# A local-attention and soft-MoE kernel: the output columns of its last stage cut into 384 and 128 in place of 256 and 256, with its steps in another order

## Chip, cores and metric

The kernel runs on one core of one Trainium2 chip. The metric is the device time of one execution in microseconds (us), from the runtime's own measurement; lower is better. Three runs of the kernel before took 188.71 to 189.39 us, with a median of 188.79 us. The core has a matrix engine (TensorE: PE for matmuls, PEld for loading their stationary operand), three engines for elementwise work (VectorE = DVE, ScalarE = ACT, GpSimd = POOL), a queue engine that issues transfers (SyncE = SP) and 16 DMA engines that carry them. Matmuls write PSUM (8 banks of 128 x 512 float32 here), all else lives in SBUF (128 partitions).

## What is computed

Attention with 8 heads over 4 sequences of 768 tokens, where a key is kept if it is one of the first 8 or one of the last 96, with a linear bias by distance; its output, as 3072 tokens of 512 features, goes through a soft mixture of 8 experts with 4 slots each. Only the mixture's end is touched here:

```python
logits = x @ phi                          # 3072 x 32
d = softmax(logits, axis=0)
slot_input = (d.T @ x).reshape(8, 4, 512)
for e in range(8):
    h = np.maximum(slot_input[e] @ w1[e], 0.0)     # 4 x 1024
    slot_out[e] = h @ w2[e]                        # 4 x 512
c = softmax(logits, axis=1)
return c @ slot_out.reshape(32, 512)      # 3072 x 512
```

All is float32. `w1` and `w2` are 16.8 MB each and are read once; the output is 6.29 MB.

## The kernel before

Up to about 136 us the kernel works through 16 units of attention, in the order of the table `ORDER`, while the weights stream into whatever SBUF is free. Then comes a tail that is written out by hand, in the order in which the code stands:

- `Moe.hidden` (line 104): the first projection and its relu, 64 matmuls of 512 columns, four at a time side by side in the array (one per slot of four experts: 128 rows, 32 columns of weights each).
- `Moe.project` (line 144): the second projection, `h @ w2`. It is done in two parts of the 512 output columns, `OUT_PART` (line 45). Part 0 gathers in bank `xx[:, 0]`, part 1 in `xx[:, 1]`. A part has 16 rounds (two halves `a` of the experts, eight chunks `c` of the inner dimension); a round is four matmuls side by side, with the part's width as their moving columns. The trace shows each float32 matmul as two records, so that a round is two passes of four.
- `weights_by_slot` (line 169): seven transposes turn the token weights `c` into `ct`; DVE copies them out of PSUM.
- `slots_raw` (line 179) copies a part's slots out of PSUM (ACT), `slots_spread` (line 183) repeats them over the four groups of 32 partitions with a matmul (tile `sp`) and copies them to `sos`.
- `combine` (line 193): one step is `c @ slot_out` for `k` tiles of 128 tokens in each of four groups, in four PSUM banks `cp`; ACT and DVE copy two banks each to SBUF, and SP issues one output transfer for each pair of banks. `STEPS` (line 46) is the number of tiles in each step.

Small PSUM tiles come from six banks in turn (`LeftBanks`), so a step waits for the copies out of the bank that it takes again. `load_w` (line 399) issues the weights. The last eight pieces of the 32 (24 to 31, the second half of `w2`) go into buffers that still hold first-projection weights, so `reuse_first` and `reuse_second` are called from inside `hidden` and issue them in columns as they come free. All transfers, weights and output, go through SP's one queue in program order, and eight may be outstanding. The fallback `general` is taken only if a flag is set; every engine reads the flag (line 968) and branches at the end.

Of the kernel before, what the change touches and what calls it, by code (L numbers as in the profile page):

```python
# [20 lines left out]
B, H, S, D = 4, 8, 768, 64  # L21
# [3 lines left out]
P = 128  # L25
NJ = 7
# [15 lines left out]
E, SPE, DF = 8, 4, 1024  # L42
NS = E * SPE
HF = DM // 2
OUT_PART = ((0, HF), (HF, HF))
STEPS = ((1, 1, 2, 2), (1, 1, 2, 2))
XH = NJ * HF
TABW = 4 * QW
NW = 10
# [17 lines left out]
class Moe:  # L67
# [69 lines left out]
    def segments(n, c):  # L137

        at, w = OUT_PART[n]
        f = 8 * at + c * w  # L140
# [37 lines left out]

    def slots_raw(self, o, ow):

        self.nc.scalar.copy(out=ow, in_=o[:, 0:ow.shape[1]])

    def slots_spread(self, ps, ow, so, copies):

        nc = self.nc
        m = ow.shape[1] // 2
        for k, copy in enumerate(copies):
            sp = ps.tile([P, 512], F32, name="sp", tag="x")
            c = slice(m * k, m * k + m)
            nc.tensor.matmul(out=sp[:, 0:m], lhsT=self.spread, rhs=ow[:, c], start=True, stop=True)  # L190
            copy(out=so[:, c], in_=sp[:, 0:m])  # L191

    def combine(self, ps, ct, n, so, obs, out, step):


        nc = self.nc
        at, w = OUT_PART[n]
        k, t0 = STEPS[n][step], sum(STEPS[n][:step])
        cps = [ps.tile([P, 512], F32, name="cp", tag="x") for _ in range(B)]
        for h in range(k):  # L200
            for b in range(B):
                r = slice(NS * b, NS * b + NS)
                t = t0 + h
                nc.tensor.matmul(out=cps[b][:, w * h:w * h + w], lhsT=ct[r, P * t:P * t + P], rhs=so[r], start=True, stop=True)  # L204
        for b in range(0, B, 2):
            obs.append(obs.pop(0))
            ob = obs[-1][:, 0:2 * k * w]
            for i, copy in enumerate((nc.scalar.copy, nc.vector.tensor_copy)):
                copy(out=ob[:, k * w * i:k * w * i + k * w], in_=cps[b + i][:, 0:k * w])
            c = B * S // P * at + w * (B * t0 + b * k)  # L210
            nc.sync.dma_start(out=out[:, c:c + 2 * k * w], in_=ob)


class BiasTable:
# [83 lines left out]
def tile_attention_moe(ctx: ExitStack, tc: tile.TileContext, qk, v, phi, w1, w2, nn, out):  # L298
    nc = tc.nc
# [28 lines left out]
    WP = 2048  # L328
    VC, VH = NJ * 2 * D, NJ * (D + 1)
    VV = VH + VC // 2  # L330
    weights = [keep.tile([P, WP], F32, name=f"wp{i}") for i in range(NW)]
# [43 lines left out]
    npl = len(places)  # L375
    extras = []
    for k, n in enumerate(held):
        at = 0
        for c0, c1 in sorted(c for h, *cs in spaces for c in cs if h == n) + [(WP, WP)]:
            if at < c0:  # L380
                extras.append((NW + k, at, c0))
            at = c1
# [4 lines left out]
    def piece(k):  # L387
        m, r = divmod(k, 16)
        if m == 0:
            a, r = divmod(r, 8)  # L390
            half, s = divmod(r, 4)
        else:
            half, r = divmod(r, 8)
            a, s = divmod(r, 4)
        return m, 4 * a + s, half
# [3 lines left out]
    def load_w(pieces, c0=0, c1=WP):  # L399

        for k in pieces:
            m, e, half = piece(k)
            nc.sync.dma_start(out=places[k][:, c0:c1], in_=(w1, w2)[m][e][:, WP * half + c0:WP * half + c1])
# [94 lines left out]
    class LeftBanks:  # L498

        n = 0  # L500
# [368 lines left out]
    ct = ts.tile([P, S], F32, name="ct")  # L869
# [7 lines left out]
    def check_inputs():  # L877

        def reduced(c, rows, x, axes, at_least):
            nc.vector.tensor_reduce(out=fl[0:rows, c:c + 1], in_=x, axis=axes, op=ALU.min)  # L880
            nc.vector.tensor_scalar(out=fl[0:rows, c:c + 1], in0=fl[0:rows, c:c + 1], scalar1=at_least, scalar2=None, op0=ALU.is_ge)

        reduced(1, KB, rsall[:, :, 0:6], AX.XY, RS_MIN)
        reduced(6, TN[6], rsall[0:TN[6], :, 6], AX.X, RS_MIN)
        xt = left.tile([P, 512], F32, name="xt", tag="x")
        nc.tensor.transpose(out=xt[0:B * H, 0:KB], in_=xmax, identity=ident[0:KB, 0:KB])  # L886
        nc.vector.tensor_reduce(out=fl[0:B * H, 5:6], in_=xt[0:B * H, 0:KB], axis=AX.X, op=ALU.max)  # L887
        nc.vector.tensor_scalar(out=fl[0:B * H, 5:6], in0=fl[0:B * H, 5:6], scalar1=X_MIN, scalar2=None, op0=ALU.is_ge)
        reduced(7, KB, cst[:, :, 1], AX.X, 0.5)
        nc.vector.tensor_scalar(out=fl[:, 2:3], in0=nlo, scalar1=1.0, scalar2=None, op0=ALU.is_ge)  # L890
        nc.vector.tensor_scalar(out=fl[:, 3:4], in0=nlo, scalar1=float(WIN), scalar2=None, op0=ALU.is_le)
        nc.vector.tensor_scalar(out=fl[:, 4:5], in0=ngl, scalar1=float(NG), scalar2=None, op0=ALU.is_le)
        nc.vector.tensor_reduce(out=fl[:, 8:9], in_=fl[:, 0:8], axis=AX.X, op=ALU.min)
        nc.vector.tensor_scalar(out=fl[:, 9:10], in0=fl[:, 8:9], scalar1=-1.0, scalar2=-1.0, op0=ALU.add, op1=ALU.mult)

    def set_flag():
        ft = left.tile([P, 512], F32, name="ft", tag="x")
        nc.tensor.matmul(out=ft[0:1, 0:1], lhsT=fl[:, 9:10], rhs=ones[:, 0:1], start=True, stop=True)
        nc.vector.tensor_scalar(out=flag[0:1], in0=ft[0:1, 0:1], scalar1=0.5, scalar2=None, op0=ALU.is_ge)
# [7 lines left out]
    w1_of = lambda e, half: places[where[0, e, half]]  # L907

    def reuse_first():
        load_w(range(npl + 1, npl + 5), 0, WP // 2)  # L910
        load_w(range(npl + 5, 31), 0, WP // 4)

    def reuse_second():
        load_w([31], 0, WP // 4)
        load_w(range(npl + 1, npl + 5), WP // 2, WP)
        load_w(range(npl + 5, 31), WP // 4, WP)

    moe.hidden(left, Moe.slot_view(sl), w1_of, hs, ht, (reuse_first, reuse_second))
    load_w([31], WP // 4, WP)

    obs = [places[16 + i // 2][:, 1024 * (i % 2):1024 * (i % 2) + 1024] for i in range(2 * (npl - 16))]
    ops = [xx[:, n] for n in range(2)]
    parts = [slice(at, at + w) for at, w in OUT_PART]

    def project(n, a, cs=range(8)):
        moe.project(ops[n], ht, lambda e, h: places[where[1, e, h]], n, a, cs)

    def weights(tiles, copy):
        moe.weights_by_slot(left, lnat, ct, [(t, TN[t], KB * t) for t in tiles], copy)

    def slots_raw(n):
        moe.slots_raw(ops[n], ows[:, parts[n]])

    def slots_spread(n, *copies):
        moe.slots_spread(left, ows[:, parts[n]], sos[:, parts[n]], copies)

    def combine(n, *steps):
        for step in steps:
            moe.combine(left, ct, n, sos[:, parts[n]], obs, out, step)

    for a in range(2):
        project(0, a, range(4))
    moe.hidden_t(left, hs, ht, 1)
    check_inputs()
    for a in range(2):
        project(0, a, range(4, 8))
    slots_raw(0)
    weights(range(4), nc.vector.tensor_copy)
    weights(range(4, NJ), nc.vector.tensor_copy)
    slots_spread(0, nc.scalar.copy, nc.scalar.copy)  # L950
    project(1, 0, (0,))
    combine(0, 0, 1)
    project(1, 0, (1, 2, 3))
    combine(0, 2)
    project(1, 0, (4, 5, 6))
    combine(0, 3)
    project(1, 0, (7,))
    project(1, 1)
    slots_raw(1)
    set_flag()  # L960
    slots_spread(1, nc.vector.tensor_copy, nc.scalar.copy)
    combine(1, *range(len(STEPS[1])))
    order.close()
    tail.close()
    banks.close()
# [7 lines left out]
def general(ctx, tc, moe, qk, v, phis, w1, w2, ngl, nlo, ident, out):  # L973
# [114 lines left out]
    with ExitStack() as g3:  # L1088
# [26 lines left out]
        obs = [sb.tile([P, 1024], F32, name=f"gob{i}") for i in range(2)]  # L1115
        for n, (at, w) in enumerate(OUT_PART):
            c = slice(at, at + w)
# [4 lines left out]
            moe.slots_spread(ps, ow[:, c], so[:, c], (nc.vector.tensor_copy, nc.scalar.copy))  # L1122
            for step in range(len(STEPS[n])):
                moe.combine(ps, ct, n, so[:, c], obs, out, step)
# [6 lines left out]
def _layout(q, k, v, n_global, n_local, moe_phi, moe_w1, moe_w2):  # L1131
# [6 lines left out]
    for j in range(NJ):  # L1138
# [11 lines left out]
        "w1": np.asarray(moe_w1, f32).reshape(E, 4, P, DF).transpose(0, 2, 1, 3).reshape(E, P, 4 * DF),  # L1150
        "w2": np.concatenate([w2[..., a:a + w].reshape(E, P, 8 * w) for a, w in OUT_PART], axis=2),
        "n": np.array([[int(n_global), int(n_local)]], np.int64).view(np.int32),
# [28 lines left out]
```

## Time and profile before

| What | Value |
|---|---|
| median of three runs | 188.79 us (188.71 to 189.39) |
| the profiled execution, its own time | 188.87 us |
| its span, first to last instruction | 186.9 us |
| outside the span in that execution | 1.97 us |
| PE busy, share of the span | 169.8 us, 91% |
| DVE, ACT, POOL busy | 142.5, 125.4, 91.6 us |
| DMA mean rate; read, written | 328 GB/s; 54.59 MB, 6.29 MB |
| granted TensorE clock, mean | 0.986 of 2.4 GHz |

Times in the rows are microseconds from the first instruction. Shares are averages over a span with very different stages, so the tail is read by itself: which engine works without a break, when the DMA engines idle, and what the last landing waits for. A matmul's end is modelled, so starts of successive rows say more than durations.

### The profile page before, as it was taken

Reading aid. Unit: us, or ns where it says so; the run is one execution under the profiler, and the core shown is the slowest. Engines: PE = TensorE matmul, PEld = TensorE weight load, DVE = VectorE, ACT = ScalarE, POOL = GpSimd, SP = SyncE. Lnnn points to the kernel's source line nnn. Section 1 sums busy time; section 2 is a strip of 40 time slices with the busy share of each in tenths; the row PEclk is TensorE's granted clock in tenths of the full one; section 3 lists DMA queues with packets and bytes.
Section 4 is the critical chain, followed back from the end, with each engine's and each line's share of the span. In section 5 each row is a group of like instructions: output and inputs, shape, how many; then the busy total and the mean of one; then the engine's idle time right before and its main releaser. Section 6 shows DMA issues by size and latency. Waiting matters only on the chain.

```text
span 186.9 us, 6377 instructions
## 1 busy us (share of the span) xinstructions
PE 169.8 (91%) x2635; PEld 123.7 (66%) x2635; DVE 142.5 (76%) x379; ACT 125.4 (67%) x161; POOL 91.6 (49%) x121
## 2 busy tenths in 40 slices
PE   8899899999998999999999997898899999998900
PEld 2568689887886798888789895584523355554600
DVE  5999999999999999899999899974687002541610
ACT  3499989999987989999999999924102111341610
POOL 6826688868967769569769776700010000000000
PEclk9999999999999999999999999999999999999995
DMA  5999999898998856988986789999999999877592
GB/s 186 419 406 391 407 404 399 335 366 273 375 361 306 329 200 199 365 282 313 312 301 176 247 297 418 349 341 412 408 375 349 404 408 420 319 295 291 222 394 83
DMA packets 14872, 61.38 MB, mean 328 GB/s; under 512 B 1650, under 2 KB 2802, under 8 KB 13042
## 3 DMA queue, kind: packets, MB, share of 16 engines
q1 hardware_dynamic: 14832, 60.89, 86.6%
q8 instruction: 22, 0.36, 0.7%
q14 instruction: 16, 0.13, 0.2%
q10 hardware_dynamic: 2, 0.00, 0.0%
HBM read 54.59 MB, written 6.29 MB: 326 GB/s over the span
## 4 chain that ended last, share of the span: by engine, by line


## 5 line engine op out<-in xcount | busy, mean ns | idle before, releaser
L581 POOL TENSOR_TENSOR ph<-tb,ph 128x432 f16<-128x432 f32 x78 | 82.3, 1085 | 28.1 <-ACT ph L574 26.4
L571 ACT ACTIVATE tb<-tb,nb 128x1296 f32<-128x1296 f32 x32 | 43.5, 1373 | 1.6 <-DVE nb L567 1.5
L598 PEld LDWEIGHTS <-ph 128*128 128x128 f16 x1248 | 41.4, 97 | 3.8 <-issue 3.2
L598 PE MATMUL x<-v,ph 128*128 128x65 f16 (+1 forms) x1248 | 43.1, 193 | 0.4
L574 ACT CAST ph<-tb 128x1296 f16<-128x1296 f32 x32 | 40.7, 1271 | 3.2 <-PE x L598 2.0
L546 PE MATMUL sc<-raw 64*128 64x216 f32 (+1 forms) x392 | 39.3, 338 | 1.2 <-DVE mx L555 1.2
L546 PEld LDWEIGHTS sc<-raw 64*128 64x128 f32 x392 | 32.3, 186 | 6.0 <-DVE mx L555 2.5
L623 DVE CUSTOM_DVE_ANT_1 xn<-x,rc 120x448 f32<-120x448 f32 x32 | 18.8, 620 | 0.6
L555 DVE CUSTOM_DVE_ANT_1 tb<-sc,tt,mx 128x864 f32<-128x864 f32 x16 | 17.8, 1114 | 1.0 <-POOL ph L581 0.4
L635 PE MATMUL m<-ident,xn 120*128 120x120 f32 x105 | 16.1, 277 | 2.1 <-DVE nb L567 1.0
L524 DVE SCALAR_TENSOR_TENSOR v<-vt,v 128x896 f16<-128x896 f32 x14 | 15.2, 1085 | 0.2
L635 PEld LDWEIGHTS m<-ident,xn 120*128 120x128 f32 x105 | 10.7, 140 | 5.6 <-DVE nb L567 1.4
L581 DVE TENSOR_TENSOR ph<-tb,ph 128x432 f16<-128x432 f32 x18 | 13.4, 760 | 0.0
L99 PE MATMUL hp<-wp,sl 128*32 128x512 f32 x80 | 10.7, 594 | 0.0
L555 DVE CUSTOM_DVE_ANT_1 tb<-sc,xtt,mx 128x864 f32<-128x864 f32 x8 | 8.9, 1112 | 0.5 <-PE sc L546 0.4
L204 PE MATMUL cp<-sos,ct 32*128 32x256 f32 x96 | 8.7, 405 | 0.5 <-ACT sos L191 0.4
L555 DVE CUSTOM_DVE_ANT_1 tb<-sc,xta,mx 128x864 f32<-128x864 f32 x8 | 8.8, 1101 | 0.1
L517 ACT ACTIVATE v<-vt 128x896 f16<-128x896 f32 x9 | 8.6, 952 | 0.0
L555 DVE CUSTOM_DVE_ANT_1 tb<-sc,tt 128x864 f32<-128x864 f32 x8 | 8.4, 1050 | 0.0
L204 PEld LDWEIGHTS cp<-sos,ct 32*128 32x128 f32 x96 | 5.7, 183 | 3.3 <-ACT sos L191 1.0
L152 PE MATMUL x<-wp,ht 128*32 128x256 f32 x128 | 7.7, 382 | 0.0
L887 DVE TENSOR_REDUCE fl<-xt 32x1 f32<-32x120 f32 x1 | 0.3, 271 | 9.3 <-PE xt L886 9.3
(212 smaller groups left out, 267.2 us busy)
## 6 DMA issues: line engine op xcount, KB each, us to landing
raw<-in_qk_dram SPq DMA_DIRECT2D x14, 832.0 KB, 5.9
wp<-in_w_dram SPq DMA_DIRECT2D x10, 1024.0 KB, 8.0
vt<-in_v_dram SPq DMA_DIRECT2D x14, 448.0 KB, 5.3
wp<-in_w_dram SPq DMA_DIRECT2D x8, 512.0 KB, 8.1
tb<-in_w_dram SPq DMA_DIRECT2D x3, 1024.0 KB, 7.4
wp<-in_w_dram SPq DMA_DIRECT2D x4, 768.0 KB, 11.7
out_dram<-ph SPq DMA_DIRECT2D x4, 512.0 KB, 4.7
wp<-in_qk_dram SPq DMA_DIRECT2D x2, 832.0 KB, 9.4
```

The lines of the kernel that those rows point to most:

```text
L99: self.nc.tensor.matmul(out=hp[n][32 * s:32 * s + 32, :], lhsT=slv(a, c, s), rhs=w1(4 * a + s, c // 2)[:, (c % 2) * DF + 512 * n:(c % 2) * ...
L204: nc.tensor.matmul(out=cps[b][:, w * h:w * h + w], lhsT=ct[r, P * t:P * t + P], rhs=so[r], start=True, stop=True)
L517: nc.scalar.activation(out=vhi[u % 2][:, :, :, 0:D], in_=vraws(u), func=AF.Copy, scale=V_SC)
L524: nc.vector.scalar_tensor_tensor(out=vlo[k].rearrange("p j i d -> p (j i) d"), in0=vraws(u).rearrange("p j i d -> p (j i) d"), scalar=V_SC ...
L546: nc.tensor.matmul(out=z[:, i, at:at + n], lhsT=r_[r, KCOL[j]:KCOL[j] + KR], rhs=r_[r, KW + KB * j:KW + KB * j + n], start=True, stop=True)
L555: nc.vector.tensor_tensor_reduce(out=tb(u)[:, :, BW * k:BW * k + BW], in0=sc[(3 * u + k) % 2][:, :, 0:BW], in1=table.unit(u % NP, k), scal ...
L571: nc.scalar.activation(out=t, in_=t, func=AF.Exp, bias=nbs[u], scale=T_SC)
L574: nc.scalar.copy(out=blocks(phi_[i])[:, :, 0:QW], in_=tb(u)[:, i].rearrange("p (s c) -> p s c", c=QW))
L581: (engine or nc.gpsimd).tensor_tensor(out=blocks(plo_[i])[:, c, 0:QW], in0=tb(u)[:, i].rearrange("p (s c) -> p s c", c=QW)[:, c], in1=bloc ...
L598: nc.tensor.matmul(out=x[:, (D + 1) * t:(D + 1) * t + d], lhsT=w[:, c:c + P], rhs=vv[:, j, i, 0:d], start=(z == 0), stop=(z == len(ops) - ...
L623: nc.vector.tensor_tensor_reduce(out=xnb[(u // 2) % 3][:, :, c:c + D], in0=xv[:, i, :, 0:D], in1=rcs.pop((u, i)).unsqueeze(2).to_broadcast ...
L635: nc.tensor.transpose(out=m[:, at:at + KB], in_=xnb[(u // 2) % 3][:, t, P * (p % 2):P * (p % 2) + P], identity=ident[0:KB, 0:KB])
```

## The change

The columns are cut into 384 and 128. A combine step now names its columns too: part 0 has four steps over its first 256 columns and two over the other 128, part 1 has two steps of three tiles. Rounds of the second part are run between part 0's steps in groups of 2, 2, 4 and 8; the transposes of the token weights stand ahead of the second half of part 0; `slots_spread` takes three copies for part 0 and one for part 1, and part 1's stands behind the fourth combine step. The flag is set early. The weights' columns are issued in halves of a piece. The output's layout in memory follows the blocks, and the host puts it together.

```diff
-OUT_PART = ((0, HF), (HF, HF))
-STEPS = ((1, 1, 2, 2), (1, 1, 2, 2))
+OUT_PART = ((0, 384), (384, 128))
+STEPS = (((0, 256, 0, 1), (0, 256, 1, 1), (0, 256, 2, 2), (0, 256, 4, 2), (256, 128, 0, 4), (256, 128, 4, 2)),
+         ((0, 128, 0, 3), (0, 128, 3, 3)))
...
     def slots_raw(self, o, ow):
 
-        self.nc.scalar.copy(out=ow, in_=o[:, 0:ow.shape[1]])
+        w = ow.shape[1]
+        for c in (slice(0, min(w, HF)), slice(HF, w))[:1 + (w > HF)]:
+            self.nc.scalar.copy(out=ow[:, c], in_=o[:, c])
...
-        m = ow.shape[1] // 2
+        m = ow.shape[1] // len(copies)
...
-        at, w = OUT_PART[n]
-        k, t0 = STEPS[n][step], sum(STEPS[n][:step])
+        f, w, t0, k = STEPS[n][step]
...
-                nc.tensor.matmul(out=cps[b][:, w * h:w * h + w], lhsT=ct[r, P * t:P * t + P], rhs=so[r], start=True, stop=True)
+                nc.tensor.matmul(out=cps[b][:, w * h:w * h + w], lhsT=ct[r, P * t:P * t + P], rhs=so[r, f:f + w], start=True, stop=True)
...
     def reuse_first():
-        load_w(range(npl + 1, npl + 5), 0, WP // 2)
-        load_w(range(npl + 5, 31), 0, WP // 4)
+        load_w(range(npl + 1, 31), 0, WP // 2)
 
     def reuse_second():
-        load_w([31], 0, WP // 4)
-        load_w(range(npl + 1, npl + 5), WP // 2, WP)
-        load_w(range(npl + 5, 31), WP // 4, WP)
+        load_w(range(npl + 1, npl + 3), WP // 2, WP)
 
     moe.hidden(left, Moe.slot_view(sl), w1_of, hs, ht, (reuse_first, reuse_second))
-    load_w([31], WP // 4, WP)
+    load_w([31], 0, WP // 2)
+    load_w(range(npl + 3, 32), WP // 2, WP)
...
+    def project_rounds(first, past):
+        for k in range(first, past):
+            project(1, k // 8, (k % 8,))
 
     for a in range(2):
         project(0, a, range(4))
     moe.hidden_t(left, hs, ht, 1)
     check_inputs()
+    weights(range(4, NJ), nc.vector.tensor_copy)
+    weights(range(4), nc.vector.tensor_copy)
     for a in range(2):
         project(0, a, range(4, 8))
     slots_raw(0)
-    weights(range(4), nc.vector.tensor_copy)
-    weights(range(4, NJ), nc.vector.tensor_copy)
-    slots_spread(0, nc.scalar.copy, nc.scalar.copy)
-    project(1, 0, (0,))
+    set_flag()
+    project_rounds(0, 2)
+    slots_spread(0, nc.scalar.copy, nc.vector.tensor_copy, nc.scalar.copy)
+    project_rounds(2, 4)
     combine(0, 0, 1)
-    project(1, 0, (1, 2, 3))
+    project_rounds(4, 8)
     combine(0, 2)
-    project(1, 0, (4, 5, 6))
+    project_rounds(8, 16)
+    slots_raw(1)
     combine(0, 3)
-    project(1, 0, (7,))
-    project(1, 1)
-    slots_raw(1)
-    set_flag()
-    slots_spread(1, nc.vector.tensor_copy, nc.scalar.copy)
-    combine(1, *range(len(STEPS[1])))
+    slots_spread(1, nc.vector.tensor_copy)
+    combine(0, 4, 5)
+    combine(1, 0, 1)
```

On PE, in the middle of part 0's projection, `htp` is the transpose of the hidden values' second half, `xt` belongs to the test of the inputs, `ctp` are the token weights and `x` is the projection's bank. Before:

```order
L132 MATMUL htp<-ident,wp_89 128x128 x4
L886 MATMUL xt<-ident,xmax 32x120
L152 MATMUL x<-tb_95,ht 32x256
L152 MATMUL x<-v_100,ht 32x256
L152 MATMUL x<-tt,ht 32x256
L152 MATMUL x<-ph_99,ht 32x256
```

After:

```order
L135 MATMUL htp<-ident,wp_89 128x128 x4
L890 MATMUL xt<-ident,xmax 32x120
L178 MATMUL ctp<-ident,lnat 128x120 x2
L178 MATMUL ctp<-ident,lnat 128x48
L178 MATMUL ctp<-ident,lnat 128x120 x4
L155 MATMUL x<-tb_95,ht 32x384
L155 MATMUL x<-v_100,ht 32x384
```

The seven `ctp` transposes, which stood behind the projection, moved in front of its second half, whose rounds are half again as wide.

On PE at the end of part 1's projection, its last round and what follows it (`sp` the slots spread, `cp` the combine steps, `ft` the flag). Before:

```order
L152 MATMUL x<-wp_87,ht 32x256
L152 MATMUL x<-wp_88,ht 32x256
L152 MATMUL x<-wp_90,ht 32x256
L152 MATMUL x<-wp_91,ht 32x256
L898 MATMUL ft<-ones,fl 1x1
L190 MATMUL sp<-ows,spread 128x128 x2
L204 MATMUL cp<-sos,ct 128x256 x24
```

After:

```order
L155 MATMUL x<-wp_87,ht 32x128
L155 MATMUL x<-wp_88,ht 32x128
L155 MATMUL x<-wp_90,ht 32x128
L155 MATMUL x<-wp_91,ht 32x128
L209 MATMUL cp<-sos,ct 128x256 x8
L195 MATMUL sp<-ows,spread 128x128
L209 MATMUL cp<-sos,ct 128x128 x48
```

A whole combine step of part 0 now stands between the last round and the spread, and 24 of the 48 narrow matmuls behind it still belong to part 0.

SP's queue from the first output transfer on, with columns per partition. Before:

```order
L211 DMA out_dram<-tb_95 128x512 x2
L211 DMA out_dram<-v_100 128x512 x2
L211 DMA out_dram<-tt 128x1024 x2
L211 DMA out_dram<-ph_99 128x1024 x2
L968 TENSOR_LOAD flag
L968 ISA x2
L211 DMA out_dram<-xtt 128x512 x2
L211 DMA out_dram<-xta 128x512 x2
L211 DMA out_dram<-ph_98 128x1024 x2
L211 DMA out_dram<-tb_95 128x1024 x2
```

After:

```order
L215 DMA out_dram<-tb_95 128x512 x2
L215 DMA out_dram<-v_100 128x512 x2
L974 TENSOR_LOAD flag
L974 ISA x2
L215 DMA out_dram<-tt 128x1024 x2
L215 DMA out_dram<-ph_99 128x1024 x2
L215 DMA out_dram<-xtt 128x1024 x2
L215 DMA out_dram<-xta 128x512 x2
L215 DMA out_dram<-ph_98 128x768 x2
L215 DMA out_dram<-tb_95 128x768 x2
```

There are 16 transfers and 6.29 MB in both; the flag is read before the third step instead of the fifth, and the sizes of the last eight differ.

## Rows read from the trace of the kernel before

**Rows 1.** The page's head, and what was read and written.

```profile
span 186.9 us, 6377 instructions
...
HBM read 54.59 MB, written 6.29 MB: 326 GB/s over the span
```

**Rows 2.** Stretches of the tail: us, busy by engine, granted clock, DMA share, GB/s.

```profile
142.00:158.00 16.00, 15.75 (x209) 6.84 (x201) 4.05 (x17) 1.73 (x4) 0.00 (x0) 1.00 1.02 402
...
160.00:162.00 2.00, 1.98 (x24) 1.09 (x16) 0.94 (x3) 1.01 (x4) 0.00 (x0) 1.00 0.69 280
...
164.00:172.00 8.00, 7.52 (x132) 4.37 (x125) 2.72 (x5) 2.52 (x5) 0.00 (x0) 1.00 0.80 315
172.00:174.00 2.00, 1.62 (x17) 0.99 (x16) 0.68 (x3) 0.70 (x3) 0.00 (x0) 1.00 0.09 33
174.00:176.00 2.00, 1.99 (x24) 1.59 (x24) 1.54 (x5) 1.36 (x5) 0.00 (x0) 1.00 0.54 201
176.00:182.00 6.00, 1.32 (x12) 0.90 (x12) 2.16 (x4) 1.64 (x4) 0.00 (x0) 0.97 1.03 393
```

**Rows 3.** SP's last output transfer, its issue, and its time to landing.

```profile
L211 SPq DMA_DIRECT2D out_dram<-tb x1: 1109/1109/1109, 178.5 to 178.5; - x1
...
DMA to landing us min/median/max: 6.7/6.7/6.7
```

**Rows 4.** SP's timeline of output transfers: start, duration, what.

```profile
161.55 0.83 SPq L211 DMA_DIRECT2D out_dram<-tb  x2
...
165.56 0.93 SPq L211 DMA_DIRECT2D out_dram<-tt  x2
168.07 1.40 SPq L211 DMA_DIRECT2D out_dram<-ph  x2
174.10 0.81 SPq L211 DMA_DIRECT2D out_dram<-xtt  x2
```

**Rows 5.** PE's timeline of the tail: start, duration, what, idle before it.

```profile
149.95 0.38 PE L152 MATMUL x<-tb,ht 128*32 128x256 f32 x1
...
150.17 0.38 PE L152 MATMUL x<-tb,ht 128*32 128x256 f32 x1
...
153.52 0.66 PE L132 MATMUL htp<-ident,wp 128*128 128x128 f32 x4
...
154.53 0.40 PE L152 MATMUL x<-tb,ht 128*32 128x256 f32 x1 [0.25 <-ACT ht L134]
...
158.12 1.02 PE L175 MATMUL ctp<-ident,lnat 120*128 120x120 f32 x7
159.08 0.71 PE L190 MATMUL sp<-ows,spread 128*128 128x128 f32 x4
159.72 0.64 PE L152 MATMUL x<-wp,ht 128*32 128x256 f32 x8
160.29 1.95 PE L204 MATMUL cp<-sos,ct 32*128 32x256 f32 x16
162.17 1.50 PE L152 MATMUL x<-wp,ht 128*32 128x256 f32 x24
163.60 1.15 PE L204 MATMUL cp<-sos,ct 32*128 32x256 f32 x16
164.67 1.50 PE L152 MATMUL x<-wp,ht 128*32 128x256 f32 x24
...
171.09 0.19 PE L898 MATMUL ft<-ones,fl 128*1 128x1 f32 x2
171.77 0.71 PE L190 MATMUL sp<-ows,spread 128*128 128x128 f32 x4 [0.48 <-ACT ows L181]
```

**Rows 6.** PEld's timeline, a projection pass and two passes of the spread.

```profile
149.95 0.11 PEld L152 LDWEIGHTS x<-tb,ht 128*32 128x32 f32 x1 [0.28 <-issue]
...
159.07 0.19 PEld L190 LDWEIGHTS sp<-ows,spread 128*128 128x128 f32 x1
...
159.29 0.30 PEld L190 LDWEIGHTS sp<-ows,spread 128*128 128x128 f32 x2
```

**Rows 7.** SP's last weight load, piece 31: its issue, and its time to landing.

```profile
L403 SPq DMA_DIRECT2D wp<-in_w_dram x1: 378/378/378, 150.6 to 150.6; - x1
...
DMA to landing us min/median/max: 13.8/13.8/13.8
```

More of the change, by code (lines that the diff above doesn't have):

```diff
@@ L44 @@
 HF = DM // 2
-OUT_PART = ((0, HF), (HF, HF))
-STEPS = ((1, 1, 2, 2), (1, 1, 2, 2))
+OUT_PART = ((0, 384), (384, 128))
+STEPS = (((0, 256, 0, 1), (0, 256, 1, 1), (0, 256, 2, 2), (0, 256, 4, 2), (256, 128, 0, 4), (256, 128, 4, 2)),
+         ((0, 128, 0, 3), (0, 128, 3, 3)))
+BLOCKS = [(n, *step) for n in range(2) for step in STEPS[n]]
+BLOCK_AT = [sum(4 * w * k for _, _, w, _, k in BLOCKS[:i]) for i in range(len(BLOCKS) + 1)]
 XH = NJ * HF
@@ L196, in combine @@
         nc = self.nc
-        at, w = OUT_PART[n]
-        k, t0 = STEPS[n][step], sum(STEPS[n][:step])
+        f, w, t0, k = STEPS[n][step]
+        at = BLOCK_AT[len(STEPS[0]) * n + step]
         cps = [ps.tile([P, 512], F32, name="cp", tag="x") for _ in range(B)]
@@ L209, in combine @@
                 copy(out=ob[:, k * w * i:k * w * i + k * w], in_=cps[b + i][:, 0:k * w])
-            c = B * S // P * at + w * (B * t0 + b * k)
-            nc.sync.dma_start(out=out[:, c:c + 2 * k * w], in_=ob)
+            nc.sync.dma_start(out=out[:, at + b * k * w:at + (b + 2) * k * w], in_=ob)
 class BiasTable:
@@ L1173 @@
     y = np.empty((2, 2, S // P, P, DM), np.float32)
-    for n, (at, w) in enumerate(OUT_PART):
-        t0 = 0
-        for k in STEPS[n]:
-            c = B * S // P * at + w * B * t0
-            y[:, :, t0:t0 + k, :, at:at + w] = o[:, c:c + w * B * k].reshape(P, 2, 2, k, w).transpose(1, 2, 3, 0, 4)
-            t0 += k
+    for (n, f, w, t0, k), c in zip(BLOCKS, BLOCK_AT):
+        at = OUT_PART[n][0] + f
+        y[:, :, t0:t0 + k, :, at:at + w] = o[:, c:c + 4 * w * k].reshape(P, 2, 2, k, w).transpose(1, 2, 3, 0, 4)
     return y.reshape(B * S, DM)
```

## The prediction

> **What bounds the kernel now.** I read the stretches of the tail first [rows 2], then SP's transfers [rows 3, 4], then PE's order [rows 5]. All that is changed lies behind 149.95 us of a span of 186.9 us [rows 1]. Two things take turns there. Until about 161 us the DMA engines are full with weights (402 GB/s over 142 to 158), and PE is busy as well. From the first output transfer at 161.55 on, PE makes output more slowly than the DMA engines could take it: 315 GB/s over 164 to 172 and, worst, a share of 0.09 over 172 to 174, when part 0's output has run out and part 1's has not begun. From there on the DMA engines set the end. The first transfer of part 1 is issued at 174.10 [rows 4]; 201 GB/s over 174 to 176 is 0.40 MB, which at the later 393 GB/s takes 1.02 us, so its data start at 174.98, 0.88 us behind the issue. Half of the 6.29 MB, 3.15 MB, at 393 GB/s takes 8.0 us and ends, evenly spread, at 182.98. The last transfer is issued at 178.5 and lands 6.7 us later, at 185.2 [rows 3]: the slowest DMA engine is 2.2 us behind the mean. I call this the skew. The span ends 1.7 us after that landing. So the end is: the moment from which output runs without a gap, plus the bytes left, plus skew, plus 1.7 us. PE counts only through that moment.
>
> **The change, part by part.** The sum is made against the profiled execution's own 188.87 us (186.9 us of span and 1.97 around it), 0.08 us above the median of the three runs.
>
> *Wider rounds of part 0.* A pass of 256 columns starts 0.215 us after the one before (149.95, 150.17) [rows 5]; a round is two passes. 384 columns should cost 1.5 times that, 0.107 us more per pass, 1.72 us for eight rounds. The first eight rounds took 3.57 us (149.95 to 153.52); with 1.72 more the `htp` transposes start at 155.24.
>
> *Token weights turned earlier.* `htp` to the next round took 1.01 us, of which 0.25 us is a wait for ACT's copy of `ht`; the seven `ctp` transposes took 0.96 us (158.12 to 159.08) [rows 5]. Put in that wait, the two together take 0.76 + 0.96 = 1.72 us, so the second half of part 0 starts at 156.96: the gain is 0.25 us. DVE's copies of them have over 5 us of cover. The second half took 3.59 us; with 1.72 more it ends at 162.27, where it ended at 158.12.
>
> *From there to the first combine step.* The flag's matmul 0.19 us; two rounds of 128, priced like the one of 256 at 159.72 to 160.29, 0.57 us; the spread, 0.64 us for two pieces and 0.21 for the third, 0.85 us; again two rounds, 0.57 us. The first combine step starts at 164.45, against 160.29 [rows 5]. ACT's two copies of the raw slots lie beside the flag's matmul and two rounds, the copies of the spread beside the next two; that cover is thin, and if it failed, a wait like the 0.48 us before the spread at 171.77 would come in [rows 5]. So the first output is late by 4.16 us. This is the price of the change.
>
> *The next steps.* Two combine steps 1.88 us; four rounds of 128, 1.00 us (the 1.43 of three rounds of 256 less one of 0.43); the third step 1.07 us, from 167.33 to 168.40; eight rounds 1.43 + 0.43 = 1.86 us; the fourth step at 170.26 [rows 5]. Each such step's first transfer is issued 1.96 us after its start (163.60 to 165.56) [rows 4, 5]: 169.29 and 172.22.
>
> *From the fourth step on.* Part 1's raw slots are copied while PE still does the fourth step, so the wait of 0.48 us and the hole of 172 to 174 are gone. What remains (the fourth step's 1.05 MB, 1.57 MB of the narrow steps of part 0 and 1.57 MB of part 1) is 4.19 MB, against 3.15 before. Part 1's transfers were issued over 174.10 to 178.5, 4.4 us for 3.15 MB [rows 3, 4]. At that pace 4.19 MB from 172.22 on are issued by 178.1, 1.4 us a megabyte, while the DMA engines need 2.5: each transfer is issued before its turn, by more and more, which hides the narrower matmuls, the copy of `sos` on DVE (queued there behind the fourth step's copies) and the flag read early on SP.
>
> *When the DMA engines are full.* The third step's data start at 169.29 + 0.88 = 170.17 and take 1.05 / 0.393 = 2.67 us, to 172.84. The fourth step's would start at 173.10, 0.26 us later. From there 4.19 MB take 10.66 us: 183.76, against 182.98. **That is 0.78 us later.** The hole of two microseconds is closed, and it is paid for with four at the front.
>
> *The weights.* The bytes are the same and in one queue, so they end as before; piece 31 landed last, at 150.6 + 13.8 = 164.4 [rows 7]. Part 0 now needs three quarters of `w2` by 162.27. The last quarter-piece of that is tenth of the sixteen loads of 8.4 MB, so 3.15 MB ahead of the end, 7.8 us at 402 GB/s before 161 to 164, at 153 to 156; it is needed at about 160. Part 1's last rounds start at 168.4, against 164.4. I take nothing for it.
>
> *Narrow matmuls.* No row shows four side-by-side matmuls of 128 columns. From below, half of a 256 pass, 0.107 us; from above, stream and load one after the other, 0.11 + 0.11 = 0.22 us, with the load of 0.11 us [rows 6]. I take the lower end: the loads of the second pass start at 149.95, with the first pass's matmuls, and the passes stay 0.215 apart, so the load lies under the stream; and the spread's loads of 128 columns, each 0.19 us long, start 0.11 us apart (159.07, third at 159.29) [rows 6]. The Trainium skill ("TensorE: Matmul & The Clock Gate", Part 3, packing small matmuls) says that a load overlaps with matmuls in flight only where the row groups differ. The four matmuls of a round all use all rows, so by it the load would be paid in every pass; the trace at 256 columns doesn't agree, and at 128 no row decides. By the rule the upper end would hold, which is the third rival.
>
> Sum: 188.87 + 0.78 = 189.6 us, with skew and last 1.7 us as before; 0.4% over the median.
>
> **The rivals.**
>
> *The output runs without a gap from the start, faster.* If the small switches between steps that I carried over (about 0.12 us at each of five places) hide, and the gap of 0.26 us and that before the third step close, the 6.29 MB run in one piece: 16.0 us from 164.45 + 1.26 (160.29 to 161.55) + 0.88 = 166.59, less 0.6, ends at 182.0. With the skew of 2.2 and 1.7 the span is 185.9: 187.9 us. With the skew of the first half's output, whose last transfer of 1.40 us of issue time at 168.07 still showed 33 GB/s in 172 to 174, it may be half a microsecond less: 187.4 to 187.9, say 187.6. For it: nothing but PE's order stands between the steps. Against it: the first two steps' 1.05 MB last only 2.67 us, to 169.3, and the third step's data come at 170.2.
>
> *The skew grows, slower.* The skew of 2.2 us grew in an unbroken run of 8 us. The weights' run was longer: even at its end the share was 0.69 in 160 to 162, output included, and the last piece landed at 164.4 [rows 2, 7], about 3 us behind the mean at 161. The new run has 13.6 us without a real pause. If the skew is 3.1 us, it ends 0.9 us later: 190.5 us. It decides from a skew of 2.4 us on.
>
> *A narrow pass costs load and stream.* Then 16 rounds of 128 cost 32 x 0.11 = 3.5 us more, all ahead of the fourth step: 193.1 us. The spread's passes [rows 6] speak against it.
>
> **How the numbers follow.** The forecast, no change that can be told, 189.6 us: 0.40. Without gaps, 187.6: 0.27. Larger skew, 190.5: 0.25. Narrow passes, 193.1: 0.08. A measurement of this kernel can tell about 0.5%, 0.94 us: faster is below 187.85, slower above 189.73. The forecast stands close to the upper bound, but its own spread lies mostly below, since each carried switch counts against the change; I leave it whole in "same". The first rival is faster, the other two slower: 0.27, 0.40, 0.33. The range of 8 in 10 goes from 187.1 to 190.9; it leaves out the third rival and the edges of the others. The forecast's own range is 188.7 to 189.9.
>
> **What would show it.** The first output transfer issued near 165.7; the first narrow passes 0.107 us apart; no PE wait for a weight load; a DMA share near 1 from about 170 to 183.5; last issue near 178.1, last landing near 186.0. I am wrong if the first output comes before 165, if a wait for banks or copies appears between the steps, or if the skew at the end differs from 2.2 us.

## The result, and the profile after

The changed kernel took 190.17 us (median; 190.01 to 191.06), the kernel before 188.75 us (188.58 to 189.66) on the same chip. The ratio is 1.0064, 95% interval 1.0037 to 1.0090: slower by 0.6%, about 1.4 us (forecast: 0.8 us). The time lies inside the predicted range. The profiled execution of after took 190.67 us, half a microsecond over its median, with this head of the page:

```profile
span 188.8 us, 6508 instructions
```

Half a microsecond of it lies ahead of the changed steps on PE: the first round of the second projection starts at 150.54, against 149.95 [rows 5]. The prediction said that all that is changed lies behind 149.95; in fact the issue of the weights' columns, inside the first projection, is changed too. But seven of the nine experiments below have the first round at 149.97 to 150.00, one at 149.9 and one at 150.53, and among the seven are four with just the loads of after, so the loads don't explain the half microsecond; its cause is open. I compare the tail from that first round on. It lasted 186.9 - 149.95 = 36.95 us before and 188.8 - 150.54 = 38.26 us after: 1.31 us more, which agrees with the medians (1.42).

Stretches of the tail of after (us, busy by engine, granted clock, DMA share, GB/s), to be read against [rows 2]; the last line is a stretch of 10 us that overlaps those above it:

```profile
160.00:162.00 2.00, 2.00 (x36) 1.00 (x32) 0.00 (x0) 0.00 (x0) 0.00 (x0) 1.00 0.85 334
162.00:164.00 2.00, 1.35 (x30) 0.67 (x22) 0.14 (x1) 0.54 (x2) 0.00 (x0) 1.00 0.08 31
164.00:166.00 2.00, 2.00 (x38) 1.60 (x32) 0.29 (x1) 0.53 (x2) 0.00 (x0) 1.00 0.01 4
166.00:168.00 2.00, 1.98 (x38) 1.22 (x36) 1.51 (x4) 1.30 (x4) 0.00 (x0) 1.00 0.21 75
...
170.00:172.00 2.00, 2.00 (x66) 1.78 (x60) 0.89 (x2) 0.90 (x3) 0.00 (x0) 1.00 0.61 237
172.00:174.00 2.00, 2.00 (x32) 1.49 (x28) 1.44 (x3) 1.07 (x2) 0.00 (x0) 1.00 0.90 363
...
184.00:186.00 2.00, 0.00 (x0) 0.00 (x0) 0.00 (x0) 0.00 (x0) 0.00 (x0) 0.50 0.55 208
...
174.00:184.00 10.00, 4.02 (x90) 3.38 (x82) 4.14 (x9) 3.44 (x8) 0.00 (x0) 0.83 1.00 388
```

The old hole of 172 to 174 (0.09) is closed: 0.90 there. A new one stands at 162 to 168, between the last weights and the first output, and from 174 to 184 the DMA engines run without a gap. That is the exchange that was forecast, at a somewhat worse rate.

PE's timeline of the same tail (start, duration, what, idle before it and what ended it), to be read against [rows 5]:

```profile
155.82 0.66 PE L135 MATMUL htp<-ident,wp 128*128 128x128 f32 x4
...
156.41 1.11 PE L178 MATMUL ctp<-ident,lnat 120*128 120x120 f32 x7
...
162.65 0.19 PE L902 MATMUL ft<-ones,fl 128*1 128x1 f32 x2
163.50 0.64 PE L155 MATMUL x<-wp,ht 128*32 128x128 f32 x16 [0.65 <-ACT ows L186]
164.07 0.94 PE L195 MATMUL sp<-ows,spread 128*128 128x128 f32 x6
164.94 0.65 PE L155 MATMUL x<-wp,ht 128*32 128x128 f32 x16
165.51 1.95 PE L209 MATMUL cp<-sos,ct 32*128 32x256 f32 x16
167.39 1.08 PE L155 MATMUL x<-wp,ht 128*32 128x128 f32 x32
168.40 1.15 PE L209 MATMUL cp<-sos,ct 32*128 32x256 f32 x16
169.47 1.95 PE L155 MATMUL x<-wp,ht 128*32 128x128 f32 x64
171.36 1.15 PE L209 MATMUL cp<-sos,ct 32*128 32x256 f32 x16
```

The second line from the flag's matmul (`ft`) on is the surprise: part 1's first two rounds wait 0.65 us for ACT. What ACT does there are the two copies of part 0's raw slots:

```profile
162.90 0.54 ACT L186 COPY ows<-x 128x256 f32<-128x256 f32 x2 [6.13 <-PE ft L902]
```

They read bank 0 of the PSUM tile `xx`; the rounds write bank 1 of the same tile. SP's output transfers [rows 4] in after, the first of each of four steps:

```profile
166.77 0.82 SPq L215 DMA_DIRECT2D out_dram<-tb  x2
...
170.36 0.93 SPq L215 DMA_DIRECT2D out_dram<-tt  x2
173.32 0.93 SPq L215 DMA_DIRECT2D out_dram<-ph  x2
175.43 1.23 SPq L215 DMA_DIRECT2D out_dram<-xtt  x2
```

And SP's last output transfer with its time to landing, and SP's semaphores behind the last transfers:

```profile
L215 SPq DMA_DIRECT2D out_dram<-tb x1: 867/867/867, 181.7 to 181.7; - x1
...
DMA to landing us min/median/max: 5.1/5.1/5.1
...
L975 SPq EVENT_SEMAPHORE  x8: 17/17/17, 186.6 to 187.1; - x8
```

The last transfer, issued at 181.73, lands 5.14 us later, at 186.87; SP passes eight semaphores one after the other until 187.1, and the span ends at 188.8. The fourth step is issued at 173.32. If its data start 0.88 us later, as part 1's first did before, 4.19 MB at 0.393 MB/us end at 184.87. The slowest engine lands 2.0 us behind that (2.2 before), and the span ends 1.9 us behind the landing (1.7 before): the two together are the same. So the end follows from one moment, and I test it in this form: **the span ends some 4.8 us (0.88 + 2.2 + 1.7) behind the largest, over all steps, of "issue of the step's first transfer plus the bytes from it on at 0.393 MB/us".** Before, that is part 1's first step; in after the fourth step. The 4.8 us is measured on the kernel before alone; the table at the end of the experiments holds the sum for each run.

### The profile page after: what moved, and what is told of

Its sections match the earlier page's. It is cut to its first block, busy times and chain, and to the rows that moved or that the text cites. A ratio compares the mean times of both kernels' runs of the same rounds, so it can differ in the third digit from the quotient of the medians.

```text
span 188.8 us, 6508 instructions
## 1 busy us (share of the span) xinstructions
PE 171.6 (91%) x2699; PEld 125.1 (66%) x2699; DVE 142.9 (76%) x380; ACT 125.3 (66%) x161; POOL 91.5 (48%) x121
## 3 DMA queue, kind: packets, MB, share of 16 engines
HBM read 54.59 MB, written 6.29 MB: 322 GB/s over the span
## 4 chain that ended last, share of the span: by engine, by line
## 5 line engine op out<-in xcount | busy, mean ns | idle before, releaser
L209 PE MATMUL cp<-sos,ct 32*128 32x128 f32 (+1 forms) x144 | 9.4, 330 | 0.8 <-ACT xtt L214 0.5
L155 PE MATMUL x<-wp,ht 128*32 128x128 f32 (+2 forms) x176 | 8.1, 323 | 0.7 <-ACT ows L186 0.7
L209 PEld LDWEIGHTS cp<-sos,ct 32*128 32x128 f32 x144 | 7.0, 185 | 2.5 <-ACT xtt L214 0.6
```

## The experiments

Each run was timed beside the kernel before on the same chip.

**Two tiles for the two banks.** Only the place of the projection's two sums is changed: two PSUM tiles of a bank each instead of two halves of one tile.

```diff
-    psx = banks.enter_context(tc.tile_pool(name="psx", bufs=1, space=PSUM))
+    xst = ExitStack()
+    psx = xst.enter_context(tc.tile_pool(name="psx", bufs=1, space=PSUM, side="right"))
...
-    ops = [xx[:, n] for n in range(2)]
+    xst.close()
+    psy = banks.enter_context(tc.tile_pool(name="psy", bufs=1, space=PSUM, side="right"))
+    ops = [psy.tile([P, 512], F32, name=f"y{n}", tag=f"y{n}") for n in range(2)]
```

> The changed kernel with the two parts of the second projection in two PSUM tiles of one bank each, in place of the two halves of one tile; all else as in the changed kernel (190.17 us). What it takes away is PE's wait of 0.65 us for ACT's copy of part 0's slots, ahead of the first rounds of part 1. Theory (whatever delays the first outputs delays the end, because the transfers run without a pause from the fourth step on): 0.6 us less, 189.5 to 189.7. Rival (the end is set by the transfers' bytes and by the slowest DMA engine, so half a microsecond on PE is swallowed): no difference, 190.1 to 190.3.

Measured: 189.5 us, ratio 1.0036 (1.0018 to 1.0053), as the theory had it. PE's timeline at the place of the wait:

```profile
162.10 0.17 PE L903 MATMUL ft<-ones,fl 128*1 128x1 f32 x1
162.10 0.31 PE L155 MATMUL y<-wp,ht 128*32 128x128 f32 x3
162.13 0.16 PE L903 MATMUL ft<-ones,fl 128*1 128x1 f32 x1
162.15 0.60 PE L155 MATMUL y<-wp,ht 128*32 128x128 f32 x13
162.77 0.94 PE L195 MATMUL sp<-ows,spread 128*128 128x128 f32 x6
```

The rounds now start with the flag's matmul, and the copies lie beside them. Everything behind comes 0.74 us sooner, counted from the first round, the end too (37.52 against 38.26). So the wait was the two halves of one tile standing in order, not the bank that was read, and it is paid in full. But 0.36% of loss is left.

**The weights turned late.** The `ctp` transposes go back behind the second half of part 0, as in the kernel before; all else as in after.

```diff
-    weights(range(4, NJ), nc.vector.tensor_copy)
-    weights(range(4), nc.vector.tensor_copy)
     for a in range(2):
         project(0, a, range(4, 8))
     slots_raw(0)
     set_flag()
+    weights(range(4, NJ), nc.vector.tensor_copy)
+    weights(range(4), nc.vector.tensor_copy)
```

> The changed kernel with one part undone: the seven transposes of the token weights stand behind the copy of part 0's slots again, as before the change, and no longer in the wait for ht. Theory (the transposes are better used as cover for the copy of the slots, 0.65 us of wait, than for the wait of ht, 0.25 us): first rounds of part 1 start 0.4 to 0.5 us earlier, 189.6 to 189.8. By the prediction's own sum (turning them early gains 0.25 us): 190.4. If the front does not matter: 190.2.

Measured: 190.03 us, ratio 1.0057 (1.0040 to 1.0074), which can't be told from after's 1.0064; the expected 189.6 to 189.8 was missed. PE's timeline:

```profile
161.47 0.19 PE L902 MATMUL ft<-ones,fl 128*1 128x1 f32 x2
161.60 1.17 PE L178 MATMUL ctp<-ident,lnat 120*128 120x120 f32 x7
162.70 0.64 PE L155 MATMUL x<-wp,ht 128*32 128x128 f32 x16
```

The transposes fill the time in which the rounds would have waited, and the wait is gone. Counted from the first round, the flag's matmul comes 0.63 us sooner than in after (11.48 against 12.11) and the rounds 0.25 us sooner (12.71 against 12.96). So with one tile for both banks, turning the weights early lost a little: without the wait of 0.65 us after's rounds would have started at 12.31, 0.40 us ahead of the 12.71, and the wait that it uncovered took back more than that.

**After without the fourth step's two transfers.** The computation is whole, but 1.05 MB of output (the first 256 columns of token tiles 4 and 5) are not written.

```diff
-            nc.sync.dma_start(out=out[:, at + b * k * w:at + (b + 2) * k * w], in_=ob)
+            if (n, step) != (0, 3):
+                nc.sync.dma_start(out=out[:, at + b * k * w:at + (b + 2) * k * w], in_=ob)
```

> The changed kernel without the two output transfers of its fourth combine step (1.05 MB are not written; everything is computed and copied as before). Theory (DMA engines are full from this step to the end): 1.05 MB at 0.39 MB/us less, 2.6 to 2.7 us, 187.4 to 187.7. Rival (PE and the copies set the end, and the transfers keep up with them): 190.0 to 190.2.

Measured: 190.06 us, ratio 1.0074 (1.0045 to 1.0103), no gain against after in the times; counted from the first round the end came 0.56 us sooner in the profiled execution, where I had expected more. The stretches show why: the hole is back.

```profile
172.00:174.00 2.00, 2.00 (x36) 1.82 (x38) 1.49 (x3) 1.06 (x2) 0.00 (x0) 1.00 0.64 258
174.00:176.00 2.00, 1.54 (x30) 1.28 (x24) 1.82 (x4) 1.65 (x4) 0.00 (x0) 1.00 0.20 76
```

My theory named the step that decides and forgot the one next in line. The fifth step is issued 24.89 us behind the first round, with 3.15 MB left: 24.89 + 8.00 = 32.89, only 0.56 below the fourth's 33.45, and the end is 0.56 sooner.

**Before without the same transfers.** The same edit in the kernel before; again 1.05 MB are not written.

> The kernel before without the two output transfers of its fourth combine step (1.05 MB are not written; everything is computed and copied as before). Theory (these transfers end in front of the hole at 172 to 174 us, in which the DMA engines idle): no difference, 188.5 to 188.8. Rival (the bytes of the output set the end in this kernel too): 2.6 us less, 186.1.

Measured: 189.17 us, ratio 1.0013 (0.9994 to 1.0032): no difference, as expected, since part 1's first step decides there. The profiled execution ended 0.55 us later behind its sum than the kernel before did, with less to write. Some 0.3 us of it lie in the last transfer, which took 7.0 us from its issue to its landing, against 6.7 [rows 3]. Why is open, and it marks how much the 4.8 us can vary.

**The column split alone undone.** Halves of 256 again, with the rest of after's order on PE (token weights turned early, early flag, rounds in groups of 2, 2, 4 and 8) and the two tiles. With the halves go three things that the cut below leaves out: the steps of the kernel before, its issue of the weights' columns, and two copies of part 0's spread in place of three.

```diff
-OUT_PART = ((0, 384), (384, 128))
+OUT_PART = ((0, 256), (256, 256))
...
-    combine(0, 4, 5)
-    combine(1, 0, 1)
+    combine(1, 0, 1, 2, 3)
```

> The column split alone undone: halves of 256, everything else as in after (early weights, early flag, rounds in groups of 2, 2, 4 and 8) with the two banks in two PSUM tiles. Theory: first output at 12.7 behind the first round, fourth step's at 21.7, 21.7 + 10.67 = 32.3; the end 37.1, a time of 189.0 us, ratio 1.001, against 1.0036 with the split. If the split as such cost the whole 0.6 us of the two-tile kernel over the kernel before, or more, then 188.4 us or less.

Measured: 189.01 us, ratio 0.9996 (0.9981 to 1.0012), end 37.02 behind the first round: as expected to 0.1 us. Against the two-tile kernel (1.0036) the split, with those three things, costs 0.4%.

**The rounds spread out, at three widths.** Part 0's combine in six steps of one token tile, with two or three of the second projection's rounds between each two, for first parts of 256, 320 and 384 columns, with the two tiles. The order against after is shown; the columns and the list of steps change with it, and at 256 and 320 the weights' columns and the copies of part 0's spread are those of the run above:

```diff
-    combine(0, 0, 1)
-    project_rounds(4, 8)
+    combine(0, 0)
+    project_rounds(4, 6)
+    combine(0, 1)
+    project_rounds(6, 8)
     combine(0, 2)
-    project_rounds(8, 16)
+    project_rounds(8, 10)
+    combine(0, 3)
+    project_rounds(10, 13)
+    combine(0, 4)
+    project_rounds(13, 16)
     slots_raw(1)
-    combine(0, 3)
+    combine(0, 5)
```

> As the run with 320 and 192, but in halves of 256 as in the kernel before: the column split undone, with the early weights, the early flag, the two tiles and the rounds between single steps kept. Theory: first combine at 11.4 behind the first round, first output at 12.6, 12.6 + 16.0 = 28.6; part 1's first output at 21.9, 21.9 + 8.0 = 29.9; the end 34.7, a time of 186.5 us, ratio 0.988: the order alone brings it, not the split. If what pays is the wider first part, it lies near the kernel before, 188.9 us.

> Columns in parts of 320 and 192, two banks in two PSUM tiles, part 0's combine in six steps of one token tile (all 320 columns) with two or three rounds of the second projection between each two. Theory (the span ends 4.81 us behind the largest of 'issue of a step plus the bytes from it on at 0.393 MB/us'): counted from the first round, half a part costs 4.4 us, the first combine starts at 12.6, the first output at 13.85; 13.85 + 16.0 = 29.85; part 1's first output at about 22.3, 22.3 + 6.0 = 28.3; the end is 34.7 behind the first round, a span of 184.6 and a time of 186.5 us, ratio 0.988. Rival (the skew grows with an unbroken run of output): the run of 16 us shows a skew nearer 3.1 than 2.2 us, time 187.4 us. Rival (the six PSUM banks, not the order of rounds, pace the steps of one tile): part 1's first output after 25, time over 188.

> As the run with 320 and 192, but with 384 and 128. Theory: first output at 15.6 behind the first round, 15.6 + 16.0 = 31.6, no later step later than its turn; the end 36.4, a span of 186.4 and a time of 188.2 us, ratio 0.997, that is 1.1 us less than the same split in two PSUM tiles with the order of after. If the late start of output is not what the time hangs on, it is as fast as the run with 320, 186.5 us.

Measured: 188.5 us, ratio 0.9979 (0.9962 to 0.9996) at 256; 188.57 us, 0.9987 (0.9962 to 1.0011) at 320; 188.77 us, 0.9995 (0.9977 to 1.0013) at 384. All three are better than after, but the first two missed 186.5 by two microseconds, and the third missed 188.2 by half of one. At 256 PE was slower than I had priced it:

```profile
161.34 0.71 PE L209 MATMUL cp<-sos,ct 32*128 32x256 f32 x8
161.98 1.07 PE L155 MATMUL y<-wp,ht 128*32 128x256 f32 x16
162.98 0.71 PE L209 MATMUL cp<-sos,ct 32*128 32x256 f32 x8
...
172.34 3.16 PE L209 MATMUL cp<-sos,ct 32*128 32x256 f32 x36 [0.57 <-DVE sos L196]
```

A step of one tile took 0.64 us (161.34 to 161.98), not 0.55, and two rounds 1.00 us, not 0.89: each stretch of one kind of matmul took about a tenth more than I had priced it, and ten such stretches lie between the start of the first step and that of the sixth. Part 1's first combine step then waited 0.57 us for DVE's copy of the spread, which is queued there behind the sixth step's copies. Part 1's first output was issued at 23.61, not 21.9, and 23.61 + 8.0 = 31.6 sets the end. At 320, SP came late to the fourth step:

```profile
167.77 1.47 SPq L215 DMA_DIRECT2D out_dram<-tt  x2
170.49 0.81 SPq L215 DMA_DIRECT2D out_dram<-ph  x2
```

DVE's two copies for that step run from 168.81 to 169.7:

```profile
168.81 0.89 DVE L214 COPY ph<-cp 128x320 f32<-128x320 f32 x2 [0.71 <-issue]
```

The first transfer needs only the first of them, done by some 169.3, and starts 1.2 us later. In between SP reads the flag, which stands in its queue just there, though its timeline doesn't list it:

```profile
L984 SPq TENSOR_LOAD <-flag x1: 763/763/763, 169.3 to 169.3; - x1
L984 SPq FUSED_REGOPS  x1: 186/186/186, 170.1 to 170.1; - x1
L984 SPq SEQ_ASSERT  x1: 28/28/28, 170.3 to 170.3; - x1
```

At 384 the flag's read (168.60 to 169.74) delays the third step in the same way, by 1.1 us. It is not what the runs lost. Without it the next largest sum would decide: at 320 part 1's first step, 24.83 + 6.00 = 30.83 in place of 30.96, and at 384 the first step, 15.84 + 16.01 = 31.85 in place of 31.89. What missed at 320 is part 1's first output, at 24.83 instead of 22.3, and it came close to the mark of the rival in which the six PSUM banks pace the steps (after 25). But no row of PE carries a wait from the first of these steps to the spread of part 1 (163.26 to 172.9), so the banks did not hold PE there; behind the spread PE waits 0.74 us for DVE's copy, as at 256.

**Pairs first.** Halves of 256, part 0's combine in steps of 2, 2, 1 and 1 token tiles, with 4, 5 and 3 rounds between them; the cut below is against the run at 256 above.

```diff
-STEPS = (((0, 256, 0, 1), (0, 256, 1, 1), (0, 256, 2, 1), (0, 256, 3, 1), (0, 256, 4, 1), (0, 256, 5, 1)),
+STEPS = (((0, 256, 0, 2), (0, 256, 2, 2), (0, 256, 4, 1), (0, 256, 5, 1)),
...
     combine(0, 0)
-    project_rounds(4, 6)
+    project_rounds(4, 8)
     combine(0, 1)
-    project_rounds(6, 8)
+    project_rounds(8, 13)
     combine(0, 2)
-    project_rounds(8, 10)
-    combine(0, 3)
-    project_rounds(10, 13)
-    combine(0, 4)
     project_rounds(13, 16)
     slots_raw(1)
-    combine(0, 5)
+    combine(0, 3)
```

> As the run in halves of 256 with the rounds spread out, but part 0's combine in steps of 2, 2, 1 and 1 token tiles with 4, 5 and 3 rounds between them, so that PE changes over less often and a pair of tiles costs 1.0 us, not twice 0.64. Theory, with the pieces measured in that run: behind the first round, first combine 11.35 and first output 13.3, 13.3 + 16.0 = 29.3; third step's output 18.8, 18.8 + 10.67 = 29.5; fourth's 20.8, 20.8 + 9.33 = 30.1; part 1's first 22.3, 22.3 + 8.0 = 30.3; largest 30.3, where the run with single steps had 31.6; with 5.0 us behind it (4.6 to 5.4 in the runs so far) the end is 35.3, a span of 185.3 and a time of 187.2 us, ratio 0.991. Rival (with the gaps mostly closed something other than PE's order holds the end, so that all orders come out at 188.5 to 188.8): ratio 0.998.

Measured: 187.85 us (187.5 to 188.09) beside 189.06 for the kernel before, ratio 0.9938 (0.9924 to 0.9952). It missed both the expected 0.991 and the rival's 0.998. This version beats both kernels, and since the run in halves with the order of after (0.9996) shares all with it but part 0's steps and the rounds between them, the gain is that order's. PE's timeline:

```profile
161.32 1.15 PE L209 MATMUL cp<-sos,ct 32*128 32x256 f32 x16
162.39 1.93 PE L155 MATMUL y<-wp,ht 128*32 128x256 f32 x32
164.26 1.15 PE L209 MATMUL cp<-sos,ct 32*128 32x256 f32 x16
165.33 2.37 PE L155 MATMUL y<-wp,ht 128*32 128x256 f32 x40
167.63 0.71 PE L209 MATMUL cp<-sos,ct 32*128 32x256 f32 x8
...
171.62 4.62 PE L209 MATMUL cp<-sos,ct 32*128 32x256 f32 x48 [0.57 <-DVE sos L196]
```

A pair of tiles costs 1.07 us, and part 1's first output is issued at 22.91 (expected 22.3, kernel before 24.15). The end comes 1.3 us sooner than before, counted from the first round.

**All runs in one table.** All in us behind the first round, from the profiled executions; the sum is the issue of the deciding step plus its remaining bytes at 0.393 MB/us. The spans are given to 0.1 us, so the last two columns hold to about 0.05 us.

| kernel | first output | deciding step, issue | bytes from it, us | sum | end | behind the sum |
|---|---|---|---|---|---|---|
| before | 11.60 | part 1's first, 24.15 | 8.00 | 32.15 | 36.95 | 4.80 |
| after | 16.23 | fourth, 22.78 | 10.67 | 33.45 | 38.26 | 4.81 |
| after, two tiles | 15.49 | fourth, 22.04 | 10.67 | 32.71 | 37.52 | 4.81 |
| after, weights late | 15.98 | fourth, 22.53 | 10.67 | 33.20 | 38.01 | 4.81 |
| after without fourth step's transfers | 16.23 | fifth, 24.89 | 8.00 | 32.89 | 37.70 | 4.81 |
| before without the same | 11.60 | part 1's first, 24.14 | 8.00 | 32.14 | 37.50 | 5.36 |
| 256, order of after | 12.60 | fourth, 21.71 | 10.67 | 32.38 | 37.02 | 4.64 |
| 256, spread out | 12.61 | part 1's first, 23.61 | 8.00 | 31.61 | 36.61 | 5.00 |
| 320, spread out | 14.17 | fourth, 19.96 | 11.00 | 30.96 | 36.37 | 5.41 |
| 384, spread out | 15.84 | third, 19.88 | 12.01 | 31.89 | 36.73 | 4.84 |
| 256, pairs first | 13.36 | part 1's first, 22.91 | 8.00 | 30.91 | 35.63 | 4.72 |

Over the eleven kernels the sum moves by 2.5 us and the end by 2.6, and what lies behind it stays within 4.64 and 5.41. Of the first output alone nothing can be read: it is latest in after and earliest in before, but the kernel with pairs first starts output 1.8 us later than before and ends 1.3 us sooner.

## Why the prediction was right and where it was wrong

*What sets the end: right.* The end is the moment from which output runs without a gap, the bytes left, the skew and the last 1.7 us. In after that moment is the fourth step's, as forecast, with 4.19 MB and 388 GB/s over 174 to 184; skew and last stretch were 2.0 and 1.9 us, where the sum had 2.2 and 1.7. The table carries the sum through all the runs, to 0.7 us.

*Wider rounds: right.* Half of part 0 to the `htp` transposes took 155.82 - 150.54 = 5.28 us; the sum had 5.29.

*Weights turned early: right in size, without effect.* From `htp` to the flag's matmul the sum had 7.03 us, the trace 6.83. The run with the weights turned late shows that the wait that follows ate it, and 0.25 us more.

*To the first combine step: this step failed.* The prediction said that ACT's two copies of the raw slots "lie beside the flag's matmul and two rounds". They don't: those rounds write the other half of the tile that ACT reads, and wait. The working asked whether the cover was long enough, and not whether the covering work was free to run; it named "a wait like the 0.48 us" for the case, and 0.65 came. In the kernel before nobody met it, since the transposes and the spread stood between the copies and part 1's first round [rows 5]. That the two parts are halves of one tile stood in the code. With the 0.2 us that the rounds ahead were quicker, the first combine started 14.97 us behind the first round, not 14.50.

*Third and fourth step: right, late by the same half.* The fourth step started 20.82 behind the first round (forecast 20.31) and its first transfer was issued at 22.78 (22.27). So the tail grew by 1.31 us where the sum had 0.78, and the difference of 0.53 is the wait less what the rest was quicker. In the two-tile kernel, which lacks the wait, the tail is 0.57 us longer than before, and that is within 0.2 us of the sum.

*Later steps hidden: right, and thinner than it sounded.* In after the third step's sum is 19.82 + 13.34 = 33.16 and the fifth's 24.89 + 8.00 = 32.89, close below the fourth's 33.45. The forecast priced one moment and left out how close the next ones stood. Its pace of issue was wrong: the last transfer was issued not at 178.1 but at 181.73, 3 us later even when the later first round is taken off, at 2.0 us a megabyte and not 1.4. So the transfers were not ahead of their turn "by more and more", but by 0.6 us at the fifth step, 1.9 at the sixth, 0.8 and 1.3 at the last two. The wait that the prediction named as a sign of being wrong also came between the steps: PE waits 0.46 us at 175.27 for ACT's copy out of a bank. It stayed hidden, since the fifth and later steps' sums lie below the fourth's.

*Weights: right.* No wait of PE for a load shows in after's tail.

*Narrow rounds: right.* Eight rounds of 128 columns, two passes each, took 171.36 - 169.47 = 1.89 us: 0.118 us a pass, where the lower bound was 0.107 and the upper 0.22. The weight loads of those rounds:

```profile
169.47 1.69 PEld L155 LDWEIGHTS x<-wp,ht 128*32 128x32 f32 x64 [0.33 <-issue]
```

They are busy for 1.69 of the 1.89 us and PE for all of it, so load and stream overlap. By the rule in the Trainium skill ("TensorE: Matmul & The Clock Gate", Part 3) that a load overlaps with matmuls in flight only where the row groups differ, the load would be paid in each pass, since all use all row groups; the trace disagrees, and the third rival falls with it.

*The rivals.* The time lies nearest to the second (190.5), but not for its reason: the skew did not grow (2.0 us), though output ran without a gap for ten microseconds. The time lies outside the forecast's own range (188.7 to 189.9); that the wider range of 8 in 10 holds it is luck, since its upper end came from this rival. The gap-free rival was refuted by the rows: 0.61 of DMA share in 170 to 172, where the second step's data have ended and the third's, issued at 170.36, have not begun. "Same" had the largest chance; with 0.64% the result lies just beyond the 0.5% that was drawn for it, and its interval reaches to both sides of that line.

*Why the change as a whole doesn't pay.* It moves the moment from which output is unbroken from part 1's first step to the fourth, 1.4 us sooner (24.15 to 22.78), but with 1.05 MB, 2.67 us, more left behind it. To gain, the steps in the middle would have to come sooner as well, and all of them stand behind a first part that is 3.4 us longer (twice the 1.72 of the sum). The run with pairs first moves part 1's own first step ahead by 1.24 us and leaves its bytes as they are, and that is what shows in the time.

## What to carry to other kernels

Where a tail is bound by stores, write for every step the issue of its first store plus the bytes from there on; the largest sum sets the end, and an edit pays by what it takes from that one sum, down to the next. Before work is counted as cover for a copy, look whether the two touch the same tile: two banks in one tile stand in order like one. And when rounds are moved between steps, count the changes from one kind of matmul to the other: here two tiles in one step cost 1.07 us and in two separate steps 1.28.

## What the runs showed of the hardware that was not expected

The constant behind the sum was 4.8 us, to the 0.05 us that the spans allow, in five kernels (before, after, and three of its variants), and 4.64 to 5.41 in the others.

The first two combine steps of one tile each cost PE 1.88 us, the pair of tiles behind them 1.07 us, for the same sixteen matmul passes. PEld's timeline of after shows half of the reason:

```profile
165.51 0.73 PEld L209 LDWEIGHTS cp<-sos,ct 32*128 32x128 f32 x12 [0.20 <-ACT sos L196]
166.66 0.39 PEld L209 LDWEIGHTS cp<-sos,ct 32*128 32x128 f32 x4 [0.42 <-ACT tb L214]
...
168.40 0.74 PEld L209 LDWEIGHTS cp<-sos,ct 32*128 32x128 f32 x16 [0.20 <-issue]
```

Two single steps back to back take eight banks where the pair takes four, and the last of them wait until ACT has copied the first step's out (0.42 us of the 0.81). The other half follows from the same lack: with two banks free at a time the second step's matmuls run two side by side instead of four, in four half-filled passes (from 166.04, 166.26, 166.66 and 166.99), where four at a time need two. PE's own timeline hides this, since its row runs through from 165.51 for 1.95 us. The same lies in the kernel before, and the version with pairs first doesn't pay it in part 0.
